# A recurrence, two mixtures of experts' products and a gated network on one core: the recurrence's first 14 chunks issued in a written order, loads without pads, one-hot rows by scalar operations

## The chip, the core and the metric

The kernel runs on one core of one Trainium2 chip. Its engines are PE (matrix products; PEld is its weight load), DVE (vector), ACT (scalar), POOL (GpSimd) and SP, which here only issues DMAs. The metric is the device time of one execution in microseconds, as a median of runs. A stage means a stretch of the span of one profiled execution.

## The reference

Three networks follow one another. The first is a gated linear recurrence over 768 steps in each of 4 x 8 heads of width 48; its output, 3072 rows of 384, goes through a top-2 mixture of 8 experts and then through a gated network.

```python
for t in range(S):
    state = f[:, :, t, :, None] * state + einsum('bhd,bhe->bhde', k[:, :, t], v[:, :, t])
    y[:, :, t] = einsum('bhd,bhde->bhe', q[:, :, t], state)
...
noisy_logits = x @ w_gate + log1p(exp(x @ w_noise)) * noise
top2 = argpartition(-noisy_logits, 2, axis=1)[:, :2]
out[mask] += top2_w[mask, k, None] * (maximum(x[mask] @ w1[e], 0.0) @ w2[e])
...
xn = x / sqrt(mean(x * x) + 1e-06) * rms_g
return (silu(xn @ w_gate) * (xn @ w_val)) @ w_out
```

## The kernel before

**The recurrence** is cut into 24 chunks of 128 steps, six for each batch; c is a chunk's place in its batch. Heads lie in pairs, 48 rows and 16 rows of pad for each, so that a chunk's keys and queries (tile kq) fill 128 partitions. `decay` clips the logits of the gates (tile ft, L331, DVE), takes two ACT functions and one DVE scan, which gives the running sums cs. `prep` makes the scaled keys KT and queries QT from cs (two ACT exponentials, one DVE product each; odd chunks' QT is POOL's). On PE a chunk has these steps, in this order: `scores` (masked on DVE into AM), `keys` of the next chunk (turned, evacuated by ACT to Ks), `rows` of the chunk before (its output and logits; ACT evacuates and SP stores x), `inter` (queries times the carried state Ss), a product of the identity with Ss (L395), which puts the old state into the sum of `state`, and `attend` (evacuated by ACT to yT). `carry` (L409) multiplies that sum by the chunk's decay on DVE and so makes the next Ss. A batch's first chunk has no `inter`, its last no `state`, and the `keys` of the last aren't needed.

**The experts.** The first 1024 tokens (chunks 0 to 7) are routed as soon as their rows are there: `router(0, NTA)` runs in nine steps between the chunks, popped by `safe()` three times in each iteration of `gla_stream`, from iteration 8 on. Its one-hot rows r_ol and r_rh are made for eight columns at a time (L541 to L545). The list of tokens (stoka) then feeds eight indirect DMAs on POOL (`fetch`, L721) for expert 0, four for each of two tiles; DVE turns each tile, ACT and DVE split it in two halves, and only then does the first product of an expert run (L645). From there the experts' units are woven between the steps of chunks 14 to 23, and go on alone afterwards. The other 2048 tokens are routed by the same code in 15 steps, one after each unit.

**Weights** come by SP (`start_loads`, L255) and are split in halves, whi by ACT (L209) and wlo by POOL (L211). Expert 0 has eight such parts, taken by `take_part` at the ends of iterations 6 to 13.

**What sets the order.** PE issues in the order in which the kernel is written, over the whole program. DVE, ACT and POOL do so only in the start, up to the first iteration; within the loop a scheduler puts their instructions in order when the kernel is built, by priority and readiness. Each engine then issues in that order and waits in it. SP issues DMAs in its own order; one that has to wait holds those behind it. Tiles with a fixed number of buffers (ft and kq have four) make a load wait until the last reader of its buffer is done. `paced` lets a fetch wait for the latest evacuation, and for the last `tick` (AM, yT or x) as long as there was none.

## Time and profile before

| | us |
|---|---|
| median of 3 runs (1107.76 to 1109.94) | 1109.58 |
| the profiled execution | 1118.4 |
| its span, first to last instruction | 1116.6 |
| PE busy (95% of the span) | 1060.1 |
| DVE busy (60%) | 666.1 |
| ACT busy (43%) | 482.1 |
| POOL busy (31%) | 350.5 |

The profiled execution took 0.8% longer than the median. Spans of 100 us are read from its trace as they stand. The chain that ended last is PE for 43% of the span, with the products of L645 for 42%; every other line in it holds 1% or less. A line of busy time by stretch shows how many microseconds each engine worked in it, the granted share of PE's full clock of 2.4 GHz (a mean of 1.00 and 0.50 within the stretch), the mean busy share of the 16 DMA engines and their rate. In a timeline the first number is the start and the second the duration; brackets give the engine's idle time before the instruction and what ended it.

### The profile page before, as it was taken

To read this page: it belongs to the slowest core of one execution; us is meant where nothing else is said; L and a number is where in the kernel's file an instruction comes from. 1 tells how busy PE (TensorE), PEld (TensorE's weight loads), DVE (VectorE), ACT (ScalarE), POOL (GpSimd) and SP (SyncE) were. 2 spreads that over 40 slices of the span, in tenths; PEclk is the share of its full clock that TensorE was granted. 3 is DMA by queue.
4 is the path that set the end of the run, shared out by engine and by line. 5 is a ranking of instruction groups with operands and counts; after the bars stand their busy time and mean duration, and the time that the engine had idled before them with its cause. 6 is when DMAs were issued, how large, how long until landed. Compare 5 with 4: busy or idle time off the path is not lost. (4 is left out here: it accounts for less than half of the span.)

```text
span 1116.6 us, 18933 instructions
## 1 busy us (share of the span) xinstructions
PE 1060.1 (95%) x7089; PEld 959.3 (86%) x7089; DVE 666.1 (60%) x1488; ACT 482.1 (43%) x1092; POOL 350.5 (31%) x373
## 2 busy tenths in 40 slices
PE   6986899989999999999999999999999999999997
PEld 4776698878989999999898988788888888888886
DVE  6886576498777654555675769735345444353332
ACT  6764555454565443444453555423223223232211
POOL 3553343344353434545545434120030020110000
PEclk8988899999999999999999999999999999999999
DMA  9996353456776543444443534120020110110000
GB/s 293 288 276 203 116 178 123 147 163 190 249 242 212 180 127 105 134 157 120 136 148 112 159 118 133 47 69 17 1 85 1 35 51 1 57 29 1 29 1 31
DMA packets 105255, 132.96 MB, mean 119 GB/s; under 512 B 9087, under 2 KB 81171, under 8 KB 105155
## 3 DMA queue, kind: packets, MB, share of 16 engines
q1 hardware_dynamic: 95587, 112.25, 31.6%
q0 software_dynamic: 9568, 19.43, 6.3%
q8 instruction: 57, 0.93, 0.4%
q14 instruction: 43, 0.35, 0.1%
HBM read 107.63 MB, written 24.02 MB: 118 GB/s over the span
## 5 line engine op out<-in xcount | busy, mean ns | idle before, releaser
L645 PE MATMUL bank<-xhi,whi 128*128 128x256 f32 (+8 forms) x1008 | 339.6, 337 | 14.5 <-DVE hlo L750 10.3
L645 PE MATMUL bank<-xlo,whi 128*128 128x256 f32 (+8 forms) x1008 | 336.2, 334 | 1.6 <-DVE xlo L633 1.6
L645 PE MATMUL bank<-xhi,wlo 128*128 128x256 f32 (+8 forms) x1008 | 335.8, 333 | 0.0
L645 PE MATMUL bank<-whi,hhi 128*128 128x384 f32 (+2 forms) x728 | 247.6, 340 | 4.2 <-ACT y L766 2.1
L645 PE MATMUL bank<-whi,hlo 128*128 128x384 f32 (+2 forms) x728 | 245.6, 337 | 0.0
L645 PE MATMUL bank<-wlo,hhi 128*128 128x384 f32 (+2 forms) x728 | 245.0, 337 | 0.0
L645 PEld LDWEIGHTS bank<-xhi,whi 128*128 128x128 f32 x1008 | 191.2, 190 | 39.4 <-DVE hlo L750 14.7
L645 PEld LDWEIGHTS bank<-xlo,whi 128*128 128x128 f32 x1008 | 191.2, 190 | 18.4 <-DVE xlo L633 2.7
L645 PEld LDWEIGHTS bank<-xhi,wlo 128*128 128x128 f32 x1008 | 191.4, 190 | 17.3
L721 POOL DMA_INDIRECT xg<-xd,stokr x139 | 135.6, 975 | 153.9 <-ACT hhi L749 124.3
L750 DVE SCALAR_TENSOR_TENSOR hlo<-bank,hhi 128x256 fp32r<-128x256 f32 (+7 forms) x192 | 83.2, 434 | 113.8 <-ACT hhi L749 96.0
L209 ACT ACTIVATE whi<-raw 128x256 fp32r<-128x256 f32 (+1 forms) x320 | 127.7, 451 | 40.1 <-DMA raw<-in_moe_w_dram 31.5
L645 PEld LDWEIGHTS bank<-whi,hhi 128*128 128x128 f32 (+2 forms) x728 | 133.4, 183 | 10.0 <-ACT y L766 2.7
L645 PEld LDWEIGHTS bank<-wlo,hhi 128*128 128x128 f32 (+2 forms) x728 | 133.4, 183 | 6.3
L211 DVE TENSOR_TENSOR wlo<-raw,whi 128x256 fp32r<-128x256 f32 (+1 forms) x282 | 126.6, 484 | 18.1 <-ACT whi L209 10.1
L645 PEld LDWEIGHTS bank<-whi,hlo 128*128 128x128 f32 (+2 forms) x728 | 132.8, 182 | 3.4
L749 ACT ACTIVATE hhi<-bank 128x256 fp32r<-128x256 f32 (+7 forms) x192 | 74.4, 388 | 131.9 <-PE bank L645 114.7
L840 DVE TENSOR_TENSOR sg<-bank,sg 128x512 f32<-128x512 f32 x72 | 49.7, 690 | 119.5 <-ACT sg L839 119.5
L791 POOL DMA_INDIRECT xg<-yd,slots x40 | 44.3, 1108 | 242.6 <-ACT hhi L843 207.6
L839 ACT ACTIVATE sg<-bank 128x512 f32<-128x512 f32 x72 | 43.2, 600 | 145.5 <-PE bank L645 136.8
L843 ACT ACTIVATE hhi<-sg 128x512 fp32r<-128x512 f32 x72 | 45.4, 631 | 115.8 <-DVE sg L841 115.6
L721 POOL DMA_INDIRECT xg<-xd,stoka x64 | 69.5, 1086 | 60.2 <-ACT hhi L749 47.7
(160 smaller groups left out, 1098.2 us busy)
## 6 DMA issues: line engine op xcount, KB each, us to landing
raw<-in_moe_w_dram SPq DMA_DIRECT2D x64, 768.0 KB
kq<-in_kq_dram SPq DMA_DIRECT2D x23, 512.0 KB
yd<-y SPq DMA_DIRECT2D x48, 192.0 KB
ft<-in_f_logit_dram SPq DMA_DIRECT2D x23, 256.0 KB
Vs<-in_v_dram SPq DMA_DIRECT2D x24, 192.0 KB
xd<-x SPq DMA_DIRECT2D x24, 192.0 KB
raw<-in_moe_w_gate_dram SPq DMA_DIRECT2D x6, 768.0 KB
raw<-in_moe_w_val_dram SPq DMA_DIRECT2D x6, 768.0 KB
```

The costliest lines, as they stand in the source:

```text
L209: nc.scalar.activation(hi[:, j], raw[:, j], AF.Copy)
L211: e.tensor_tensor(lo[:, j], raw[:, j], hi[:, j].bitcast(F32), op=OP.subtract)
L645: nc.tensor.matmul(o, a, b, start=start and i == 0, stop=stop and i == 2)
L721: paced(nc.gpsimd.indirect_dma_start(out=b.xg[i][:, k_], out_offset=None, in_=table, in_offset=bass.IndirectOffsetOnAxis(ap=rows_of[:, k_, ...
L749: mark[0] = nc.scalar.activation(hhi[:, :N], p[:, :N], AF.Relu).ins
L750: mark[1] = nc.vector.scalar_tensor_tensor(hlo[:, :N], p[:, :N], 0.0, hhi[:, :N].bitcast(F32), op0=OP.max, op1=OP.subtract).ins
L791: paced(nc.gpsimd.indirect_dma_start(out=y, out_offset=None, in_=ya if n < GROUP else yd, in_offset=bass.IndirectOffsetOnAxis(ap=at_, axis ...
L839: nc.scalar.activation(sg, ps[0], AF.Sigmoid)
L840: nc.vector.tensor_tensor(sg, ps[0], sg, op=OP.mult)
L843: mark[0] = nc.scalar.activation(hhi, sg, AF.Copy).ins
```

## The change

For the first 14 iterations PE, ACT, DVE and POOL each issue an iteration's instructions in the order in which they are written. That order is new: `prep` of chunk i+2 is spread over the iteration's steps, the gates of chunk i+4 and the sums of i+3 come at its end, the clip of chunk i+5 goes to POOL, and the part of the weights follows as the last. All QT are DVE's. The product of the identity with Ss is gone; `carry` adds the old state on DVE (su) and multiplies by the decay on POOL, or on DVE alone for a batch's first chunk. Loads of ft and kq leave the pads out once each of their five and four buffers has been filled, with two DMAs instead of one. The first weight loads go from iterations 4 and 6 to 2 and 4, the noise from 4 to 3, the zeros for the unused slots from 3 to 18. One-hot rows are made column by column with scalar operations on DVE, two for each column; the first router has two groups of eight columns as before, the second eight groups of four instead of four of eight, so that it has 19 steps. Idle places in the first router's plan are moved: step 8 comes one place later, in the middle of iteration 11. A fetch no longer waits for a tick.

```diff
-    NK, NV = AHEAD + 1, LOADS + 2
+    NK, NV = AHEAD + 1, 5
...
+    NF, NQ = 5, 4
+    Fs = [gp.tile([P, HP, P], F32, name=f"Fs{i}") for i in range(NF)]
+    Qs = [gp.tile([P, HP, 2, P], F32, name=f"Qs{i}") for i in range(NQ)]
+    def spans(first_round):
+        return [slice(0, P)] if first_round else [slice(0, D), slice(64, 64 + D)]
     def load_f(n, cuts=WHOLE):
         b, c = divmod(n, NCH)
-        t = st["f", n] = ld.tile([P, HP, P], F32, name="ft", bufs=4)
+        t = st["f", n] = Fs[n % NF]
         for s in cuts:
-            nc.sync.dma_start(t[:, s], f_logit[b, s, :, c * P:(c + 1) * P].rearrange(
-                "a d t -> d a t"))
+            for o in spans(n < NF):
+                nc.sync.dma_start(t[o, s], f_logit[b, s, o, c * P:(c + 1) * P].rearrange(
+                    "a d t -> d a t"))
 
     def load(n, which=("kq", "v")):
         b, c = divmod(n, NCH)
-        if which != ("v",):
-            st["kq", n] = ld.tile([P, HP, 2, P], F32, name="kq", bufs=4)
         for nm in which:
             if nm == "v":
                 nc.sync.dma_start(Vs[n % NV][:, :DM], v[b, c * P:(c + 1) * P])
             else:
-                i = {"k": slice(0, 1), "q": slice(1, 2), "kq": slice(0, 2)}[nm]
-                nc.sync.dma_start(st["kq", n][:, :, i], kq[b, :, i, :, c * P:(c + 1) * P].rearrange(
-                    "a i d t -> d a i t"))
-    def steps(fn, n, cuts=WHOLE):
+                t = st["kq", n] = Qs[n % NQ]
+                for o in spans(n < NQ):
+                    nc.sync.dma_start(t[o], kq[b, :, :, o, c * P:(c + 1) * P].rearrange(
+                        "a i d t -> d a i t"))
...
+    def clip(n, s=slice(0, HP), e=None):
 
 
         f = st["f", n][:, s]
+        (e or nc.vector).tensor_scalar(f, f, -GATES_MAX - 1.5, None, op0=OP.max)
+    def gates(n, s=slice(0, HP)):
         if s.start == 0:
             st["L", n] = wk.tile([P, HP, P], F32, name="L")
+        f, l = st["f", n][:, s], st["L", n][:, s]
+        nc.scalar.activation(l, f, AF.Exp, scale=-1.0)
+        nc.scalar.activation(l, l, AF.Ln, bias=1.0)
+    def sums(n, s=slice(0, HP)):
+        if s.start == 0:
             st["cs", n] = wk.tile([P, HP, P], F32, name="cs", bufs=4)
-        l, cs = st["L", n][:, s], st["cs", n][:, s]
-        nc.vector.tensor_scalar(f, f, -GATES_MAX - 1.5, None, op0=OP.max)
-        yield
-        nc.scalar.activation(l, f, AF.Exp, scale=-1.0)
-        yield
-        nc.scalar.activation(l, l, AF.Ln, bias=1.0)
-        yield
-        nc.vector.tensor_tensor_scan(cs.rearrange("p a t -> p (a t)"),
+        nc.vector.tensor_tensor_scan(st["cs", n][:, s].rearrange("p a t -> p (a t)"),
...
-        e = nc.gpsimd if n % 2 and banks[0] is BANK and n > 1 else nc.vector
-        e.tensor_tensor(st["QT", n][:, s], cs, st["kq", n][:, s, 1], op=OP.mult)
+        nc.vector.scalar_tensor_tensor(st["KT", n][:, s], Ek, KEYS_MAX, st["kq", n][:, s, 0],
+                                       op0=OP.min, op1=OP.mult)
+        yield
+        nc.scalar.activation(cs, cs, AF.Exp, scale=-1.0)
+        yield
+        nc.vector.tensor_tensor(st["QT", n][:, s], cs, st["kq", n][:, s, 1], op=OP.mult)
...
         st["pU", n] = pU = cut(bank("U"), HP, D)
-        if c:
-            nc.tensor.matmul(pU, ident, Ss[c % 2][:, :, :D], start=True, stop=False,
-                             skip_group_check=True)
         for a in range(HP):
             for g in range(2):
                 h = 2 * a + g
                 nc.tensor.matmul(pU[64 * g:64 * (g + 1), a], Ks[n % NK][:, h],
-                                 Vs[n % NV][:, h * D:(h + 1) * D], start=not c,
-                                 stop=True, skip_group_check=True)
+                                 Vs[n % NV][:, h * D:(h + 1) * D], start=True, stop=True,
+                                 skip_group_check=True)
 
     def carry(n):
 
         c = n % NCH
         if c == NCH - 1:
             return
-        st["C"] = nc.vector.tensor_tensor(Ss[(c + 1) % 2][:, :, :D], st["pU", n],
-                                          st["cs", n][:, :, P - 1:].to_broadcast([P, HP, D]),
-                                          op=OP.mult).ins
+        u, sn = st["pU", n], Ss[(c + 1) % 2][:, :, :D]
+        w = st["cs", n][:, :, P - 1:].to_broadcast([P, HP, D])
+        if c:
+            t = wk.tile([P, HP, D], F32, name="su", bufs=1)
+            nc.vector.tensor_tensor(t, u, Ss[c % 2][:, :, :D], op=OP.add)
+            st["C"] = nc.gpsimd.tensor_tensor(sn, t, w, op=OP.mult).ins
+        else:
+            nc.vector.tensor_tensor(sn, u, w, op=OP.mult)
...
-        hlf = rp.tile([P, 2, 2 * ng], F16, name="r_hf")
+        hlf = rp.tile([P, 2, 2 * ng], F32, name="r_hf")
         V.tensor_copy(hlf, hl)
         yield
         rh = rp.tile([P, 2 * ng, nst], F16, name="r_rh")
         ol = rp.tile([P, 2 * ng, P], F16, name="r_ol")
-        w = 8
+        w = 8 if n0 == 0 else 4
         for j in range(0, 2 * ng, w):
             o = slice(j, j + w)
-            V.tensor_tensor(ol[:, o], irowh[:, None, :].to_broadcast([P, w, P]),
-                            hlf[:, 1, o, None].to_broadcast([P, w, P]), op=OP.is_equal)
-            V.tensor_tensor(rh[:, o], irowh[:, None, :nst].to_broadcast([P, w, nst]),
-                            hlf[:, 0, o, None].to_broadcast([P, w, nst]), op=OP.is_equal)
-            V.tensor_tensor(rh[:, o], rh[:, o],
-                            names[:, 2 * n0 + j:2 * n0 + j + w, None].to_broadcast([P, w, nst]),
-                            op=OP.mult)
+            for k_ in range(j, j + w):
+                V.tensor_scalar(ol[:, k_], irowh, hlf[:, 1, k_:k_ + 1], None, op0=OP.is_equal)
+                m = 2 * n0 + k_
+                V.tensor_scalar(rh[:, k_], irowh[:, :nst], hlf[:, 0, k_:k_ + 1],
+                                names[:, m:m + 1], op0=OP.is_equal, op1=OP.mult)
             yield
...
-        m = mark[0] or st.get("tick")
+        m = mark[0]
         if m is not None:
...
+    ALL = {mybir.EngineType.PE, mybir.EngineType.Activation, mybir.EngineType.DVE,
+           mybir.EngineType.Pool}
     def gla_stream():
         def valid(n):
             return 0 <= n < NT
 
-        with tc.manual_schedule(engines={mybir.EngineType.PE, mybir.EngineType.Activation,
-                                         mybir.EngineType.DVE, mybir.EngineType.Pool}):
+        with tc.manual_schedule(engines=ALL):
             rest = constants()
             load_f(0, PARTS)
             next(rest)
             warm(10)
-            load(0, "kq")
+            load(0, ("kq",))
             load_f(1)
             load(0, ("v",))
-            load(1)
+            load(1, ("kq",))
             load_f(2)
+            load(1, ("v",))
+            load(2, ("kq",))
...
         for i in range(NT + 3):
             now[0] = i
             routing.extend(plan.get(i, []))
-            if i == 0:
-                for n in range(4, GATES + 1):
+            for n in ((4, 5, 6) if i == 0 else (i + 6,)):
+                if valid(n):
                     load_f(n)
-            if valid(i + GATES + 1):
-                load_f(i + GATES + 1)
-            if valid(i + LOADS):
-                load(i + LOADS)
+            if valid(i + 3):
+                load(i + 3, ("kq",))
+            if valid(i + 2):
+                load(i + 2, ("v",))
+            es = ExitStack()
+            if i < FETCH + 2:
+                es.enter_context(tc.manual_schedule(engines=ALL))
             if valid(i):
                 scores(i)
             safe()
             yield 1.1
             if i == 0:
                 run(prep, 1)
-                for n in range(2, GATES):
-                    after_prep(decay, n)
+            more = prep(i + AHEAD) if i and valid(i + AHEAD) else iter(())
+            next(more, None)
             if valid(i + 1):
                 keys(i + 1)
                 yield 1.1
+            next(more, None)
+            next(more, None)
             if valid(i - 1):
                 rows(i - 1)
             yield 1.2
             if valid(i):
                 inter(i)
             safe()
-            if valid(i + AHEAD):
-                run(prep, i + AHEAD)
+            next(more, None)
+            if i == 0:
+                run(decay, 2)
+                clip(3)
             if valid(i):
                 state(i)
-                with tc.high_priority(30):
+                with tc.high_priority(0 if i < FETCH + 2 else 30):
                     carry(i)
+            if i == 0:
+                gates(3)
+                run(prep, 2)
+                clip(4)
+            if valid(i + 4):
+                gates(i + 4)
+            if valid(i):
                 attend(i)
+            if valid(i + 3):
+                sums(i + 3)
+            if valid(i + 5):
+                clip(i + 5, e=nc.gpsimd if i < FETCH + 2 else nc.vector)
             safe()
-            if valid(i + GATES):
-                (after_prep if i < 14 else run)(decay, i + GATES)
+            if 6 <= i < 14:
+                take_part(0)
+            es.close()
             if i == 3:
+                nc.sync.dma_start(noise, moe_noise)
+                nc.sync.dma_start(gcol, moe2_rms_g)
+            if i in (2, 4):
+                start_loads()
+            if i == FETCH + 6:
                 nc.sync.dma_start(yd.rearrange("(e s) d -> s e d", e=E)[min(CAPS):],
                                   zeros[:, None, :].to_broadcast([SPAN - min(CAPS), E, DM]))
...
-            if i == 4:
-                nc.sync.dma_start(noise, moe_noise)
-                nc.sync.dma_start(gcol, moe2_rms_g)
-            if i in (4, 6):
-                start_loads()
-            if 6 <= i < 14:
-                take_part(0)
...
     def route(steps_):
-        with tc.high_priority(50):
-            return next(steps_, None)
+        return next(steps_, None)
 
     ahead = router(0, NTA, rpa)
     idle = lambda: None
-    for i in (8, 9):
+    for i in (8, 11):
         at(i, idle)
     for i in ROUTE:
         at(i, lambda: route(ahead))
+    at(9, idle)
...
-    for gap in (0, 0, 0, 0, 0, 1, 0, 0, 0, 0, 2, 1, 2, 2):
+    for gap in (0, 0, 0, 0, 0, 1, 0, 0, 0, 0, 0, 0, 0, 0, 2, 1, 2, 2):
```

## Rows read from the trace of the kernel before

**Rows 1.** Stretches: length, busy by engine (instructions), granted clock, DMA share, GB/s.

```profile
7.61:26.59 18.98, 12.35 (x131) 10.43 (x131) 13.52 (x23) 11.97 (x21) 6.54 (x21) 0.73 1.14 325
26.59:60.42 33.83, 31.57 (x430) 26.56 (x429) 28.74 (x39) 26.27 (x54) 17.13 (x21) 1.00 0.96 290
60.42:97.70 37.28, 27.91 (x321) 23.65 (x320) 31.33 (x87) 20.05 (x44) 13.93 (x17) 0.82 0.82 245
97.70:115.59 17.89, 13.00 (x156) 10.96 (x154) 10.89 (x19) 8.45 (x17) 10.35 (x10) 0.84 0.70 204
115.59:214.30 98.71, 93.45 (x979) 83.60 (x980) 60.31 (x105) 50.81 (x118) 40.43 (x47) 0.98 0.44 140
214.30:1116.60 902.30, 876.66 (x5065) 802.23 (x5063) 517.03 (x1206) 360.43 (x831) 259.96 (x239) 0.99 0.31 98
```

**Rows 2.** Timeline of PE, one chunk: start us, us, engine, line, operation, tiles.

```profile
101.75 1.16 PE L380 MATMUL scores<-QT,KT 48*128 48x128 f32 x16
102.84 0.65 PE L173 MATMUL bank<-ident,KT 128*128 128x128 f32 x4
103.33 1.04 PE L442 MATMUL bank<-columns,yT 128*128 128x112 f32 x8
104.31 1.09 PE L420 MATMUL bank<-QT,Ss 48*64 48x128 f32 x16
105.33 0.59 PE L395 MATMUL bank<-Ss,ident 128*128 128x192 f32 x2
105.85 0.67 PE L400 MATMUL bank<-Vs,Ks 128*64 128x48 f32 x16
106.35 1.05 PE L430 MATMUL bank<-AM,Vs 128*64 128x128 f32 x15
```

**Rows 3.** One line's instructions (ns minimum/median/maximum), then the timeline of both engines.

```profile
L331 DVE TENSOR_SCALAR ft<-ft x25: 293/419/1247, 3.1 to 119.8; 128x512 f32<-128x512 f32 x23, 128x256 f32<-128x256 f32 x2
30.75 1.28 POOL L359 TENSOR_TENSOR QT<-cs,kq 128x512 f32<-128x512 f32 x1
31.06 1.25 DVE L331 TENSOR_SCALAR ft<-ft 128x512 f32<-128x512 f32 x1
```

**Rows 4.** Weight halves on POOL before 115 us; a POOL copy.

```profile
L211 POOL TENSOR_TENSOR wlo<-raw,whi x20: 723/1004/1930, 42.1 to 76.5; 128x256 fp32r<-128x256 f32 x12, 128x384 fp32r<-128x384 f32 x8
7.55 0.69 POOL L107 COPY columns<-ident 128x384 f32<-128x384 f32 x1
```

**Rows 5.** Timeline of DVE, first router: step five, one-hot rows.

```profile
85.33 0.16 DVE L531 TENSOR_SCALAR r_hl<-slots 128x16 int32<-128x16 int32 x1
85.41 0.16 DVE L532 TENSOR_SCALAR r_hl<-slots 128x16 int32<-128x16 int32 x1
86.09 1.23 DVE L541 TENSOR_TENSOR r_ol<-irowh,r_hf 128x1024 f16<-128x1024 f16 x1
87.24 0.62 DVE L543 TENSOR_TENSOR r_rh<-irowh,r_hf 128x448 f16<-128x448 f16 x1
```

**Rows 6.** Groups of DVE: busy, mean ns; one scalar operation, 16 bits.

```profile
L116 DVE TENSOR_SCALAR sel<-sel,pcol 128x512 f16<-128x512 f16 x1 | 0.6, 581 | 0.0
```

**Rows 7.** Timeline from the token list to the first expert product.

```profile
97.21 0.28 DVE L611 TENSOR_SCALAR stoka<-bank,quad 128x64 int32<-128x64 f32 x1
100.45 1.41 POOL L721 DMA_INDIRECT xg<-xd,stoka  x1 [0.17 <-issue]
110.17 1.35 POOL L721 DMA_INDIRECT xg<-xd,stoka  x1 [0.30 <-issue]
115.59 0.58 PE L645 MATMUL bank<-xhi,whi 128*128 128x256 f32 x1 [1.86 <-ACT xhi L632]
```

**Rows 8.** Stretches as in group 1: second router, plain stretch.

```profile
241.00:259.00 18.00, 12.34 (x63) 11.07 (x62) 18.00 (x41) 8.07 (x21) 9.94 (x7) 0.81 0.41 125
300.00:400.00 100.00, 96.59 (x635) 93.34 (x634) 67.45 (x159) 55.22 (x147) 46.66 (x47) 1.00 0.62 203
```

**Rows 9.** Waits of PE after 116 us: us in total, times, longest.

```profile
PE bank L645 <- DVE hlo L750: 10.3, 10, 3.3
```

More of the change, by code (lines that the diff above doesn't have):

```diff
@@ L309, in steps, with run @@
+    def run(fn, n, cuts=WHOLE):
         for _ in zip(*[fn(n, s) for s in cuts]):
-            yield
-    def run(fn, n, cuts=WHOLE):
-        for _ in steps(fn, n, cuts):
-            pass
-    def after_prep(fn, n):
-        with tc.issue_after(st["e"]), tc.issue_after(st["K"]):
-            run(fn, n)
-    def decay(n, s):
+            pass
+    def clip(n, s=slice(0, HP), e=None):
         f = st["f", n][:, s]
+        (e or nc.vector).tensor_scalar(f, f, -GATES_MAX - 1.5, None, op0=OP.max)
@@ L332, in decay @@
+    def decay(n, s):
+        clip(n, s)
         yield
-        nc.scalar.activation(l, f, AF.Exp, scale=-1.0)
+        gates(n, s)
         yield
-        nc.scalar.activation(l, l, AF.Ln, bias=1.0)
+        sums(n, s)
         yield
-        nc.vector.tensor_tensor_scan(cs.rearrange("p a t -> p (a t)"),
-                                     chain[:, s].rearrange("p a t -> p (a t)"),
-                                     l.rearrange("p a t -> p (a t)"), 0.0,
-                                     op0=OP.mult, op1=OP.add)
@@ L341, in decay, with prep @@
-        yield
-    def prep(n, s):
+    def prep(n, s=slice(0, HP)):
         if s.start == 0:
@@ L383, in scores @@
         with tc.high_priority(30):
[L384 to L386 removed]
+            nc.vector.tensor_tensor(t, p.rearrange("p g a t -> p (g a) t"),
+                                    mask[:, None, :].to_broadcast([P, H, P]), op=OP.mult)
     def state(n):
[L390 to L391 removed]
+        if n % NCH == NCH - 1:
             return
         st["pU", n] = pU = cut(bank("U"), HP, D)
[L394 to L396 removed]
         for a in range(HP):
@@ L434, in attend @@
         with tc.high_priority(30):
-            st["tick"] = nc.scalar.activation(y, pY, AF.Copy).ins
+            nc.scalar.activation(y, pY, AF.Copy)
         st["yT", n] = y
@@ L443, in rows @@
         x = wk.tile([P, HP, NX], F32, name="x")
-        st["tick"] = nc.scalar.activation(x, p[:, :, :NX], AF.Copy).ins
+        nc.scalar.activation(x, p[:, :, :NX], AF.Copy)
         nc.sync.dma_start(xd[n * P:(n + 1) * P, :], x.rearrange("p a x -> p (a x)"))
@@ L1037, in gla_stream @@
             next(rest)
-        for n in range(2, LOADS):
-            load(n)
         for i in range(NT + 3):
```

16 lines of the change are left out of this document (5 added, 11 removed).

## The prediction

> **What bounds the kernel now.** I read the busy time by stretch first [rows 1]. From 115.59 us, where the first expert product runs [rows 7], to the end PE is busy for 970.11 of 1001.01 us: that part ends when PE's work does, and only less PE work or fewer PE stalls shorten it. Before 115.59 PE often waits, and the time is that of the recurrence and of the routing in front of the experts. The reader is to see four stretches there: the start up to the third chunk's scores (18.98 us), six chunks in which PE is busy for 31.57 of 33.83 us, four with the first router in which DVE is busy for 31.33 of 37.28 us and PE for 27.91 at a mean clock of 0.82, and 17.89 us from chunk 12's scores to the first expert product. After 116 us PE's largest wait is for DVE's hlo, 10.3 us in all [rows 9], and a good part of it lies in 241 to 259, where DVE is busy for 18.00 of 18.00 us with the second router's one-hot rows, and PE for 12.34 at a clock of 0.81 [rows 8].
>
> **The change, stretch by stretch.** The sum is made on the profiled execution, 1118.4 us with a span of 1116.6, and taken over to the median, 1109.58; 0.8% on a term of ten us is nothing.
>
> *The start.* The work up to chunk 2's scores is the same and DVE has it all in a row; the first round of loads keeps its pads. The zeros are gone from a stretch where the DMA share is 1.14, but the waits there are chains of DVE and ACT, so I count 0 (-1 to +1).
>
> *Six chunks bound by PE.* Its steps start at 101.75 (scores), 102.84, 103.33, 104.31, 105.33 (identity), 105.85, 106.35 (attend), and attend takes 1.05 [rows 2]: about 5.6 us a chunk, of which the identity holds 0.52. A chunk without it takes 5.07. Of six, one has no inter (1.02), one no state (0.50), one no keys (0.49), so six take 28.4 us; the old order's own floor is 28.4 + 4 x 0.52 = 30.5, and it took 33.83, with 3.3 us of waits. The new order spreads `prep` and puts the scan three chunks ahead, so some waits go: between 28.4 and 31.7, and I take 30.0, a gain of 3.8 (2.1 to 5.4). What covers it: ACT's 26.27 busy us in six chunks include weight halves, and fall with nothing; it would be next. The DMA share is 0.96 at 290 GB/s here. A chunk loads 960 KB and stores 192; without pads the loads fall to 768, so the transfers stay hidden in a stretch 11% shorter, but with little to spare. kq and ft now issue two DMAs each on SP; the SP queue stands one to three chunks ahead and hides them, unless a weight load (moved two iterations earlier) waits in front for its buffer. The noise, one iteration earlier, is hidden the same way.
>
> *Four chunks with the first router.* DVE sets the time. It loses four clips (0.42 each when alone [rows 3]), 1.7 us, and the carry's one DVE operation is replaced by one of the same shape; it gains the QT that POOL had, about 0.7 each for one or two chunks. One-hot rows: a group of eight columns takes 1.15 (starts 86.09, 87.24) and two operations of some 0.54 (0.62, less the 0.08 by which two in a row overlap) [rows 5], 2.2 us, and two groups 4.5. Now there are 16 pairs of scalar operations. Two small ones start 0.08 us apart [rows 5], the floor; 512 columns of 16 bits took 581 ns [rows 6] against 0.16 for 16 columns, which makes 0.26 for 128 and 0.19 for 56, or 0.18 and 0.11 from start to start. A pair costs 0.16 to 0.29; I take 0.24, 3.8 us. DVE's sum falls by 1.5 us. POOL's is 13.93 now and stays: two QT of 1.28 [rows 3] go, four clips and three multiplies by the decay come, and four weight parts fall here, which until now were all done by 76.5 [rows 4]. A clip on POOL has no row. A copy of 384 columns took 0.69, and part of that may be a wait, so 0.5 is the low end; the two-input QT of 512 columns took 1.28, the high end; I take 0.7, near the copy, which has one input as well. The multiply (192 columns) is below the 0.72 of the shortest wlo (256) [rows 4]; I take 0.6 (0.4 to 0.7).
>
> POOL's time isn't free to DVE. A clip on DVE that met POOL's QT took 1.25 us and ended at 32.31, 0.28 after the QT's end at 32.03 [rows 3]: it had waited for it whole. So what is written behind a weight half in time waits for it, and 32 short operations in a row can each meet one. I take 36.3 for the stretch, a gain of 1.0 (between +5, DVE's sum alone at PE's pace, and -4, if the waits fall between the short operations). The Trainium skill, SBUF — State Buffer, "SBUF: two separate sides", says that the port pair of DVE and GpSimd is locked for a whole instruction and that the loser fully blocks; that row agrees. It speaks against moving the clip: without the lock this stretch would gain some 2 us more.
>
> *From the token list to the first expert.* The list is ready at 97.21 + 0.28; the fetches start at 100.45 and 110.17 (first and eighth), so 1.39 apart, and the first product is 5.42 us after the last start [rows 7]. POOL's chain sets this. The tick's wait goes, which may save 1 to 3 us, but three halves of a weight part (0.72 each) of iteration 11 are written ahead of the first fetch, and a clip (0.7) and two halves (1.0 each, the median [rows 4]) ahead of the last. Queued behind them are the fetches, and the first expert waits for these. If the builder lets the next iteration's fetch pass a half that isn't ready, half of this vanishes. 17.89 becomes 20.4 (16.5 to 24): a loss of 2.5. The first step of the sum, the first expert's start, so falls from 115.6 to 0 + 3.8 + 1.0 - 2.5 = 2.3 us earlier, 113.3.
>
> *Chunks 14 to 23.* PE is busy for 93.45 of 98.71. Seven of the ten have the identity product: 7 x 0.52 = 3.6 us. The new carry has one more engine in its chain, POOL, which also queues the fetches of later experts, and these wait for an evacuation each; `inter` of the next chunk would wait, but it comes some expert products later. I take 3.4 (1.5 to 3.6).
>
> *The second router.* 241 to 259 loses 18.00 - 12.34 = 5.7 us of PE, and by the clock 0.19 x 18 = 3.4 more. PE was idle before its clock fell from 2.4 to 1.2 GHz for a while. A plain stretch leaves DVE 32.5 of 100 us [rows 8], with 635 products, 15 in a unit, so 42 units: 0.77 a unit. One group a unit (2.2) overdraws it by 1.4, four groups by 5.8, which is the idle time seen. Four pairs a unit cost 0.64 to 1.16: eight units are overdrawn by 0 to 3.1. At 0.24 it is 0.96 a unit, 1.5 in all, and the slack of the units in flight takes that up in part. I count a loss of 2.6 that stays, so a gain of 6.5 (2 to 9). The token lists come four units later; the weights that need them were asked for later than that. The Trainium skill, VectorE: DVE Perf Modes, "The perf-mode tier table", gives 693 ns for 2048 columns of a 16-bit scalar operation; an estimate by that page is 0.04 us for 128, so that only the starts would count, and the sum would be 1.5 us better. No row here shows that rate: 581 ns for 512 is slower.
>
> *Zeros.* They are 1536 KB on SP's queue between weight loads, at a DMA share of 0.44 and 140 GB/s; at the 290 GB/s of a full stretch they hold the queue for 5.4 us. Halves that wait for a load are hidden behind parts already split; I take -0.5 (-2 to 0).
>
> Sum: 2.3 + 3.4 + 6.5 - 0.5 = 11.7 us; 1109.6 - 11.7 = 1097.9, so 1098.
>
> **The rivals.** *POOL becomes the bound (slower).* Place: iteration 6 to the first expert. For: four things for POOL in an order that can't move within an iteration, and the lock. Against: its sum is only 13.93 of 37.28 now. Price: clips at 1.28, multiplies at 0.7, waits between the short operations. The six chunks gain 2.1, the router stretch loses 4, the fetches 6; with 2 from the second router, 2.4 from the identity and -0.5 for the zeros it is 4.0 slower: 1113.6. It decides as soon as POOL and DVE's two-input work together need over 5 us a chunk.
>
> *The front gains nothing (no change).* The first expert stays at 115.6 or comes 2 later, and pairs at 0.29 leave half of the second router's loss: -1.5 + 3.4 + 2 - 0.5 = 3.4 at best and about 1.7 in the middle: 1108. For it: the same DVE work in the same chain.
>
> *The pipeline holds (much faster).* Chunks at PE's pace: gains of 5.4, 5 and 1.4 in front, 3.6, 9 and 0: 24.4, so 1085. For it: PE's floor is 5.07 a chunk. Against: DVE's 31.33 busy us in the router stretch.
>
> **How the numbers follow.** My forecast 0.58, POOL as the bound 0.14, no change 0.15, much faster 0.13. A run of this kernel can't be told from no change within about 0.2%, 2.2 us. Faster: nearly all of the forecast (0.55), 0.13 and a third of the no-change case, 0.73 in all; within: 0.14; slower: 0.13. The forecast's terms alone range over some 1089 to 1107; to hold 8 in 10 the range takes in most of the two cases around it: 1086 to 1112.
>
> **What would show it.** In the profile after: no L395; scores of successive chunks 5.1 us apart up to the eighth; the first expert product near 113; in the second router PE idle under 2 us and its clock not at 1.2 GHz; 3.5 us less between the first expert product and the end of the recurrence. Wrong if the first expert comes after 117, with POOL busy without gaps from iteration 10 on; if PE waits for inter after 116 us; or if DVE stays full in the second router for over 18 us.

## The result, and the profile after

The changed kernel takes 1119.26 us (median of six, 1116.20 to 1120.54), the kernel before 1110.40 (1107.76 to 1111.51): a ratio of 1.0078 [1.0062, 1.0095], so 0.8% slower where 1.1% faster was forecast. Its profiled execution took 1119.37 us with a span of 1117.0, close to its median. The two profiles' spans differ by only 0.4 us, because the profiled execution of before took 1118.4, as this kernel does on three of the five chips of the experiments (medians of 1118 to 1121 us), against 1110 to 1111 on two: chips differ, and the stages below are set against further profiles of both.

Busy time by stretch, changed kernel; the stretches end at the scores of chunks 0, 2, 8 and 12, and stand against [rows 1]:

```profile
7.66:30.39 22.73, 12.88 (x130) 10.89 (x129) 13.63 (x23) 11.85 (x21) 5.89 (x22) 0.70 1.08 216
30.39:59.34 28.95, 28.75 (x422) 25.36 (x420) 23.27 (x34) 22.11 (x43) 18.67 (x19) 1.00 0.90 217
59.34:96.80 37.46, 26.52 (x315) 22.74 (x314) 32.00 (x108) 19.19 (x43) 20.94 (x23) 0.82 0.74 158
```

The first stretch is 3.8 us longer (5 to 6 in three further profiles, below), the second 4.9 shorter, the third as long as it was. The first expert product, which ended the front at 115.59 [rows 7], comes at 121.82:

```profile
121.82 0.58 PE L649 MATMUL bank<-xhi,whi 128*128 128x256 f32 x1 [13.04 <-ACT xhi L636]
```

So the front lost 6.2 us where it should have won 2.3, PE standing idle for 13.04 us at its end. What holds it up shows in the waits of SP's queue and of DVE. First the weight loads' waits before the change (20 to 116 us), then the changed kernel's (20 to 122, and DVE's from 57):

```profile
SPq L255 <- POOL hs L361: 1.2, 1, 1.2
SPq L255 <- POOL wlo L211: 0.8, 2, 0.6
```

```profile
SPq L255 <- POOL wlo L211: 16.5, 2, 8.3
SPq L255 <- POOL hs L367: 13.2, 2, 7.4
SPq L302 <- DMA raw<-in_moe_w_dram: 5.5, 3, 2.3
```

```profile
DVE KT L360 <- DMA Qs<-in_kq_dram: 9.4, 2, 5.7
```

The weight load (L255) waits 29.7 us on SP for POOL, where it waited 2.0. The timeline shows the chain twice:

```profile
63.08 2.10 POOL L211 TENSOR_TENSOR wlo<-raw,whi 128x256 fp32r<-128x256 f32 x3
65.20 0.56 SPq L255 DMA_DIRECT2D raw<-in_moe_w_dram  x1
71.36 0.82 SPq L313 DMA_DIRECT2D Qs<-in_kq_dram  x2
74.47 0.69 DVE L360 SCALAR_TENSOR_TENSOR KT<-Ek,Qs 128x512 f32<-128x512 f32 x1 [3.73 <-DMA Qs<-in_kq_dram]
...
100.51 1.00 POOL L211 TENSOR_TENSOR wlo<-raw,whi 128x256 fp32r<-128x256 f32 x1
101.53 0.55 SPq L255 DMA_DIRECT2D raw<-in_moe_w_dram  x1
108.17 1.31 SPq L313 DMA_DIRECT2D Qs<-in_kq_dram  x2
110.72 0.69 DVE L360 SCALAR_TENSOR_TENSOR KT<-Ek,Qs 128x512 f32<-128x512 f32 x1 [5.71 <-DMA Qs<-in_kq_dram]
```

POOL's weight half ends at 65.18 and 101.51; 0.02 us later SP issues the weight load that reuses its buffer, and only behind that the keys and queries; loads in between wait for the weight's landing besides (5.5 us in three). DVE needs the keys and queries one iteration later, in an order that it can't leave, and in the second case the tokens' turn for the first expert stands behind the waiting KT.

### The profile page after: what moved, and what is told of

It is laid out like the page before. It is cut to its first block, busy times and chain, and to the rows that moved or that the text cites. A ratio compares the mean times of both kernels' runs of the same rounds, so it can differ in the third digit from the quotient of the medians.

```text
span 1117.0 us, 19042 instructions
## 1 busy us (share of the span) xinstructions
PE 1050.4 (94%) x7057; PEld 954.7 (85%) x7057; DVE 673.8 (60%) x1559; ACT 482.0 (43%) x1092; POOL 371.1 (33%) x396
```

## The experiments

The theories named below: **Q**, SP's queue is held by the weight loads; **P**, POOL's clips and products set the pace; **S**, loads in two halves fill SP's queue with twice as many transfers; **T**, the bytes of the loads count; **O**, scalar one-hot operations cost more than assumed; **A**, the written order of ACT costs the start. First-expert times are compared across chips, ratios with care: the changed kernel gave 1.0067 [1.0043, 1.0092] and 1.0059 [1.0033, 1.0086] on two more chips, on both of which the kernel before takes 1110. One and the same edit (e1 and e7) gave 0.9986 on one chip and 1.0043 on another, with intervals that don't meet, so the ratios of e1 to e4 and e6, from chips on which the changed kernel wasn't timed, can't be set against these.

**Loads behind (e1 and e7).** `start_loads()` for a finished part is called after the next iteration's loads.

```diff
             if valid(i + 2):
                 load(i + 2, ("v",))
+            while owed:
+                owed.pop()
+                start_loads()
```

> One change to the changed kernel: in iterations 7 to 13 a weight load is issued behind the next iteration's loads of ft, kq and v instead of ahead of them. Theory Q (SP's queue: the weight load waits there for POOL's weight half, 29.7 us in all between 20 and 122 us, and the keys and queries stand behind it, for which DVE then waits 9.4 us): the waits of KT for kq fall from 9.4 to under 3 us, the first expert product comes from 121.8 to between 112 and 117, and the time falls by 5 to 9 us, to 1110 to 1114. Theory P (POOL's clips and products, and the port that it shares with DVE, set the pace): the first expert stays within 120 to 123 and the time within 2 us of 1119. Theory S (loads in two halves, so that the queue reaches its limit of transfers under way sooner): SP's waits for the landing of a weight load (6.4 us now) stay, and less than half of the gain of Q is seen, 1115 to 1118.

> The changed kernel, timed on the same chip as the kernel beside it: 1.004 to 1.008 of the kernel before, first expert at 121 to 123.

> The changed kernel with nothing but the weight loads of iterations 7 to 13 issued behind the next iteration's loads. Theory Q (the queue carries most of the loss): 4 to 8 us below the changed kernel on this chip, ratio to the kernel before 0.998 to 1.002, first expert at 115 to 117. Rival (the 0.9986 came from its chip, and what the queue gives back is taken by the fetches): within 2 us of the changed kernel.

Alone, e1 reached its first expert at 116.08 (ratio 0.9986 [0.9968, 1.0004], on a chip where the changed kernel wasn't timed). Side by side on another chip, the changed kernel (first row) and e7 (second):

```profile
124.05 0.58 PE L649 MATMUL bank<-xhi,whi 128*128 128x256 f32 x1 [11.72 <-ACT xhi L636]
```

```profile
117.22 0.58 PE L649 MATMUL bank<-xhi,whi 128*128 128x256 f32 x1 [11.30 <-ACT xhi L636]
```

6.8 us sooner, and DVE's wait for keys and queries is gone from the list. It stood there for the changed kernel on this chip; the weight load's own waits, e7's in the second block, stay (23.3 us) and cost the front little when nothing urgent is behind them:

```profile
DVE KT L360 <- DMA Qs<-in_kq_dram: 8.7, 2, 5.0
```

```profile
SPq L255 <- POOL wlo L211: 16.4, 2, 9.3
SPq L255 <- POOL hs L367: 6.9, 2, 3.6
```

The times are 1118.27 and 1114.71, 1.0059 and 1.0043 [1.0013, 1.0073]: 3.6 us less by the medians, 1.8 by the ratios, with intervals that overlap. Q is shown for the front; how much of the total it gives back is not.

**Pads (e2).** `spans` returns all 128 partitions, so that each load is one DMA.

```diff
-        return [slice(0, P)] if first_round else [slice(0, D), slice(64, 64 + D)]
+        return [slice(0, P)]
```

> One change to the changed kernel: every load of ft and kq takes the pads along, in one DMA, as before. Theory S (the halves hurt: twice as many transfers, 7 in an iteration instead of 5): the scores of chunk 2 come from 30.4 to 27 to 29, DVE's wait for kq falls from 9.4 to under 5, the time falls by 4 to 8 us. Theory Q: the weight load still waits for POOL's half, the keys behind it, so the time stays within 2 us of 1119. Theory T (bytes count, as the change supposes): a third more bytes in these loads make the front slower, by 2 to 6 us.

Chunk 2's scores came at 32.1, the first expert at 121.2; the waits of KT for kq vanished, but a wait of the scan took the place (4.8 us, behind POOL's Ss), and the weight load still waited 18.2 us for POOL. S foretold an earlier start, which didn't come; time on this chip equals the kernel before (1.0003 [0.9981, 1.0025]), and without the changed kernel beside it T can't be judged by time. Nor did the pads alone change: the builder put SP's DMAs in another order. The first two weight loads are issued at 20.0 and 32.6 us instead of 28.1 and 43.7, and the zeros far earlier, as the changed kernel (first) and e2 (second) show:

```profile
154.84 0.44 SPq L1110 DMA_DIRECT2D yd<-zeros  x1
```

```profile
38.91 0.43 SPq L1110 DMA_DIRECT2D yd<-zeros  x1
```

The stretch 30.4 to 59.3 tells something else, changed kernel first, e2 second:

```profile
30.40:59.30 28.90, 28.70 (x422) 25.36 (x420) 23.23 (x34) 22.07 (x43) 18.66 (x19) 1.00 0.90 217
```

```profile
30.40:59.30 28.90, 28.90 (x402) 25.66 (x401) 23.59 (x33) 21.33 (x42) 17.55 (x18) 0.95 0.99 308
```

PE is full in both. Of the 91 GB/s between them some 54 are the zeros (1536 KB in 28.9 us), so the rates don't show what the pads take. What a KB costs the 16 DMA engines does: 0.90 x 16 / 217, or 66 ns, without pads, and 51 with them (0.99 x 16 / 308), as in the kernel before (53, from the 0.96 and 290 GB/s of its six chunks [rows 1]). A chunk's 960 KB without pads so take the engines about as long as its 1152 KB with them, an estimate from these numbers; whether it is the 48 partitions or the two DMAs is not shown.

**Old one-hot rows (e3).** The three operations on many columns, in the new places (eight and four columns).

```diff
-            for k_ in range(j, j + w):
-                V.tensor_scalar(ol[:, k_], irowh, hlf[:, 1, k_:k_ + 1], None, op0=OP.is_equal)
...
+            V.tensor_tensor(ol[:, o], irowh[:, None, :].to_broadcast([P, w, P]),
+                            hlf[:, 1, o, None].to_broadcast([P, w, P]), op=OP.is_equal)
```

> One change to the changed kernel: one-hot rows again by operations on eight (first router) and four columns (second) at a time on 16-bit elements, in the same steps and places. Theory O (a scalar pair costs 0.36 us, as its starts show, not 0.24: 16 pairs take 5.9 us where two groups took 4.5, and 32 pairs 11.7 where eight half groups should take 9 to 10.5): the first router's last scores come 1 to 2 us earlier, waits of PE for hlo between 241 and 262 us fall, the time falls by 1 to 4 us. Rival (the scalar form is what eased the second router, as was forecast): slower by 2 to 5 us. Theory Q alone: within 1.5 us.

First expert at 120.4. From the 21st evacuation of a hidden tile (hlo) to the 51st, which the second router fills, it took 78.0 us; the changed kernel takes 78.7 to 79.7, the one before 79.0 to 79.8. c1, c2, b1 and b2 below, with old rows in groups of four, took 76.5 to 78.2, c3, whose units lie otherwise, 79.2. So the groups of four gain about 2, and the scalar form gives nearly all of that back: O holds by the stages; the ratio (1.0025 [1.0002, 1.0049]) has no changed kernel beside it.

**Clips on DVE (e4).**

```diff
-                clip(i + 5, e=nc.gpsimd if i < FETCH + 2 else nc.vector)
+                clip(i + 5, e=nc.vector)
```

> One change to the changed kernel: the clip of chunk i+5 on DVE instead of POOL, at the same place of the order. Theory P (a clip takes 1.48 us on POOL against 0.42 alone on DVE, and holds up what is behind it): POOL's busy time before 122 us falls by some 18 us, the first expert comes 3 to 6 us sooner, the time falls by 4 to 8 us. Theory Q: the weight half stands behind the clip on POOL, so a weight load that waits for it comes 1.5 us earlier, three times: 1 to 3 us faster. Rival (DVE is full where the router runs, and the clip belongs to POOL): slower by 1 to 3 us.

First expert at 121.3, ratio 1.0062 [1.0039, 1.0085]. From chunk 12's scores to the first expert POOL now works for 16.64 of 24.58 us, where the changed kernel's worked for 20.74 of 25.02:

```profile
96.80:121.82 25.02, 11.98 (x156) 10.71 (x153) 17.09 (x22) 13.00 (x28) 20.74 (x21) 0.70 0.59 134
```

```profile
96.77:121.35 24.58, 13.25 (x156) 11.14 (x153) 15.78 (x25) 13.04 (x28) 16.64 (x19) 0.78 0.62 137
```

The wait stays with a POOL that has time to spare: P alone explains nothing of the front. (Together with the loads it does something, below.)

**Attend early (e5).** In iteration 0 `attend(0)` is written ahead of the gates.

```diff
             if i == 0:
+                attend(0)
                 gates(3)
                 run(prep, 2)
```

> One change to the changed kernel: in iteration 0 the products of attend and their evacuation yT are written ahead of the gates of chunk 3 and the second prep, instead of behind them. Theory A (the written order of ACT is what costs the start 3.8 us: yT of chunk 0, whose products end at 17.2, stands at 24.4 behind gates that wait for two clips, and the products of rows wait for it for 3.5 us): rows starts by 19.5, the scores of chunk 2 come from 30.4 to 26 to 28, the time falls by 2 to 4 us. Rival (DVE's chain of clip, scan, keys and queries sets the start whatever ACT's order is): the scores of chunk 2 stay within 1 us of 30.4 and the time within 1 us.

The evacuation yT moved from 24.42 to 17.56, chunk 2's scores to 28.8, from 30.4 to 32.8 in the changed kernel's profiles. That is later than A's 26 to 28: from the scores of chunk 0 on it is 21.1 us, where the changed kernel takes 22.7 to 24.8 and the kernel before 18.7 to 19.0, so ACT's order is some half of the start's loss. The time stayed, 1.0059 against 1.0067 beside it, and the first expert came at 121.6. Set against the changed kernel on the same chip, e5 is 2.3 us ahead at the scores of chunk 8 (58.0 and 60.4) and 0.3 at those of chunk 12 (97.1 and 97.4), with this wait in between: A is right on the start in part, and its gain is lost again at the loads' waits.

```profile
DVE KT L360 <- DMA Qs<-in_kq_dram: 8.1, 2, 6.4
```

**Identity (e6).** The product is back, and the carry is DVE's alone.

```diff
+        if c:
+            nc.tensor.matmul(pU, ident, Ss[c % 2][:, :, :D], start=True, stop=False,
...
+        st["C"] = nc.vector.tensor_tensor(sn, u, w, op=OP.mult).ins
```

> One part of the change undone: the product of the identity with the old state is back on PE, the carry is one operation of DVE, and POOL's and DVE's two are gone. Theory I (the product costs PE 0.52 us a chunk wherever PE is the bound, which is from chunk 14 on): the stretch from the first expert's evacuation to the twentieth is 3 to 4 us longer, the first expert comes within 2 us of the changed kernel's 121.8, the time rises by 2 to 4 us. Rival (the carry over POOL hurts the front as much as the identity hurts PE): no change, within 1 us.

1130.43 us, 1.0099 [1.0077, 1.0120]. The six chunks of the second stretch took 31.41 us, all of it PE's, where four profiles of the changed kernel have 28.95 to 29.21:

```profile
33.07:64.48 31.41, 31.41 (x430) 27.25 (x428) 24.63 (x35) 22.82 (x44) 12.73 (x15) 0.97 0.79 189
```

From the first to the 21st evacuation it took 99.9 us, the changed kernel 95.5 to 99.0. So leaving out the product does gain, some 2.4 us in the six chunks and some 3 in chunks 14 to 23; what that is of the time isn't shown, since the changed kernel wasn't timed on this chip.

**Together (c1 and c2).** Loads behind, old rows and attend early in one; the clips on DVE besides in the other; the changed kernel beside them.

> The changed kernel itself once more, as the measure for the runs beside it, since chips differ. If its ratio to the kernel before is again 1.006 to 1.010, the other ratios of this study can be set against 1.0078; if it lies near 1.000 on a chip where the kernel before is slower, the gains are to be read against this run alone.

> Three changes to the changed kernel together: weight loads behind the next iteration's loads, one-hot rows as before, attend early in iteration 0. If they add up (5.7 us for the loads by the first expert's start, 1.4 for the first router's rows, 2 to 4 for the start, 1 to 2 in the second router): the first expert at 110 to 113, and the time 9 to 13 us below the changed kernel. Rival (what is gained in front is waited for in the fetches, whose chain goes by POOL): the first expert at 114 to 117, 5 to 8 us below.

> The three changes of the kernel beside it, and the clips on DVE. Theory P2 (once the loads are out of the way POOL's clip decides the first expert: behind the fetches and a weight half it comes at 110.2, gates on ACT wait for it, and the tokens' half xhi, ready to be made at 108.5, stands behind these till 113.2): 3 to 5 us below the kernel beside it, the first expert at 106 to 110. Rival (DVE is full in the router's stretch, five clips more there): no gain, within 1.5 us of it or slower.

On one chip: changed kernel 1119.55, e5 1118.90, c1 1109.40 (0.9991 [0.9964, 1.0017]), c2 1110.21 (0.9981 [0.9953, 1.0008]). Ten us come back, clear of the intervals, though e5 alone gave none. The two profiles differ by 13.7 us, of which only 3.9 lie ahead of the first expert product; 4.8 lie between the first and the 21st evacuation and 1.8 in the second router. The recurrence as a whole comes earlier, its last scores at 200.1 instead of 209.4. That the stalls lie one behind the other and each swallows what is gained ahead of it is seen in e5; how much of the ten us it explains is argued, as neither e3 nor e7 was timed on this chip. The clips bring the first expert from 117.5 to 114.7 and the time nothing. In the kernel with the loads behind, ACT's gates wait for a clip that POOL has in line after eight fetches and a weight half, and xhi waits behind the gates (e1's timeline):

```profile
107.62 1.96 POOL L211 TENSOR_TENSOR wlo<-raw,whi 128x384 fp32r<-128x384 f32 x2
107.85 0.69 DVE L736 STREAM_TRANSPOSE xt<-xg 128x384 f32<-128x384 f32 x1 [2.48 <-DMA xg<-xd,stoka]
110.15 1.48 POOL L324 TENSOR_SCALAR Fs<-Fs 128x512 f32<-128x512 f32 x1
111.67 0.63 ACT L331 ACTIVATE L<-Fs 128x512 f32<-128x512 f32 x1 [6.70 <-POOL Fs L324]
113.24 0.51 ACT L636 ACTIVATE xhi<-xt 128x384 fp32r<-128x384 f32 x1
```

**Where the two kernels differ on one chip.** Further profiles of the kernel before, and both on one chip:

> The kernel before itself, one more profiled execution. The profile that the prediction read took 1118.4 us, 0.8% above the median, and the difference of the two medians (8.9 us) does not show between the two profiles (1116.6 and 1117.0). Theory F (that execution had a slow front, and the kernel before usually reaches its first expert sooner): the first expert product comes at 107 to 111 here instead of 115.6, and the span is 1106 to 1112. Rival (the excess lay in the experts, from the clock): the first expert at 114 to 117, and the stretch behind it 990 to 996 instead of 1001.

> The kernel before once more, to tell what varies between its executions from what is fixed: by theory F its first expert product comes at 107 to 111, by the rival at 114 to 117; the scores of chunk 2, where only the written order of the start acts, should be within 0.5 us of 26.6 in both.

> The kernel before, beside a profile of the changed kernel on the same chip. Theory M (the chip's loads: the front of both kernels waits for transfers, so a chip on which these are quicker shortens the front, and more so where loads are asked for early): where the run takes 1110, the first expert comes 3 to 8 us earlier than the 114.7 to 116.3 of the three profiles so far. Theory K (the chip's clock: fewer falls of TensorE's clock): the front is within 1.5 us of 115.6, the mean clock is higher by 0.005 or more, and the stretch behind the first expert is shorter by 5 to 9. Where the run takes 1118 to 1120 again, both are as before.

> The changed kernel on the chip of the kernel beside it. If chips differ in both kernels alike, it takes 7 to 11 us more than that one, with the first expert 5 to 8 us later, the stretch from there to the twentieth evacuation 3 to 4 shorter and the second router 0 to 2 shorter, and the rest equal; if the difference of the kernels goes with the chip, it takes within 3 us of it on a chip where that takes 1118.

F falls: the first expert of the kernel before came at 116.3, 114.7 and 114.3. On one chip (1116.67 and 1124.10 us), kernel before, then changed:

```profile
114.33 0.58 PE L645 MATMUL bank<-xhi,whi 128*128 128x256 f32 x1 [2.38 <-ACT xhi L632]
```

```profile
122.11 0.58 PE L649 MATMUL bank<-xhi,whi 128*128 128x256 f32 x1 [7.02 <-ACT xhi L636]
```

The first, 21st and 51st evacuations, in the same order:

```profile
118.21 0.42 DVE L750 SCALAR_TENSOR_TENSOR hlo<-bank,hhi 128x256 fp32r<-128x256 f32 x1 [1.98 <-ACT hhi L749]
216.49 0.42 DVE L750 SCALAR_TENSOR_TENSOR hlo<-bank,hhi 128x256 fp32r<-128x256 f32 x1 [1.14 <-ACT hhi L749]
295.45 0.42 DVE L750 SCALAR_TENSOR_TENSOR hlo<-bank,hhi 128x256 fp32r<-128x256 f32 x1
```

```profile
125.83 0.42 DVE L754 SCALAR_TENSOR_TENSOR hlo<-bank,hhi 128x256 fp32r<-128x256 f32 x1 [2.58 <-ACT hhi L753]
224.80 0.42 DVE L754 SCALAR_TENSOR_TENSOR hlo<-bank,hhi 128x256 fp32r<-128x256 f32 x1 [1.14 <-ACT hhi L753]
303.69 0.42 DVE L754 SCALAR_TENSOR_TENSOR hlo<-bank,hhi 128x256 fp32r<-128x256 f32 x1
```

7.8 us lie in front and none behind: 98.3 and 99.0 us to the 21st evacuation, 79.0 and 78.9 to the 51st. All four profiles of the kernel before are of executions of 1117 to 1120 us; none shows where it saves the rest when it takes 1110. Why the kernel before takes 1110 on some chips and 1118 to 1121 on others, while the changed one takes 1118 to 1124, stays open: M and K are not told apart, since the chip on which both were profiled is not of the first kind.

**What to keep.** b1 and b2 start from the kernel before, c3 from c2.

```diff
-        if c:
+        if c and n < 14:
             nc.tensor.matmul(pU, ident, Ss[c % 2][:, :, :D], start=True, stop=False,
...
-        w = 8
+        w = 8 if n0 == 0 else 4
```

> The kernel before with two parts of the change alone: without the identity product (carry by a sum on DVE and a product on POOL), and with the second router's one-hot rows in eight groups of four columns, by the old operations on many columns. Theory I+G: 3.0 to 3.6 us less from the first expert to the twentieth unit, 1.5 to 3 less in the second router: faster than before by 3 to 7 us (0.3 to 0.6%). Rival (the scheduler puts POOL's carry behind fetches and weight halves, and inter waits): within 1.5 us of before, or slower.

> The kernel before with the identity product left out from chunk 14 on alone, where PE is the bound, and the second router's one-hot rows in eight groups of four columns by the old operations. With the identity left out everywhere the first expert came 5 to 6 us late, and the rest was 5 to 7 us shorter. Theory I+G: the first expert stays at 114 to 117, the stretch to the twentieth evacuation is 2.5 to 3.5 shorter, the second router 1.5 to 3: 4 to 7 us faster than before (0.994 to 0.996). Rival (the front came late there because of the groups or by the scheduler's mood, not because of the carry): the first expert at 119 or later, no faster than 0.998.

> The changed kernel with loads behind, one-hot rows by the old operations, attend early, clips on DVE, and the two turns of the first tokens one iteration later. Without the last, PE waited 11.3 us for the first expert, with chunk 14's other steps written behind that. Theory W (the fetches land at the same time whatever PE does, so a chunk's work goes into that wait): the first expert within 2 us of 114.7, but the end of the recurrence 3 to 5 us earlier: 3 to 5 us below the kernel without it, so 0.993 to 0.996 of the kernel before where that takes 1110. Rival (the chunk's own operations on DVE and ACT stand ahead of the turns and push them back by as much): first expert at 118 to 120, no gain.

b1, without the identity everywhere: 0.9978 [0.9962, 0.9994], first expert at 121.5: the new carry costs the front, as b2 shows, which leaves it out there. b2, the edit shown, without it only from chunk 14 on: first expert at 115.3, 1113.68 against 1119.09 us, 0.9947 [0.9923, 0.9972]. c3, with the turns of the first tokens one iteration later: first expert at 120.3, as its rival said, yet the recurrence's last scores at 197.9 (201.4 in c2, 202.5 to 204.6 before the change), 1112.56 us, 0.9948 [0.9930, 0.9967]; c2 wasn't timed beside it. Both are 0.5% faster than the kernel before on the same chip, where the changed kernel's one run took 1124.10. On a chip where the kernel before takes 1110 neither was timed.

## Why the prediction was wrong

**The start: wrong.** I counted 0 (-1 to +1) and it lost 3.8; in the three further profiles the stretch took 24.0 to 24.8 us, for 18.7 to 19.0 before, with a mean granted clock of 0.53 to 0.65 (0.73 before [rows 1]). I said that the work was the same and that DVE had it in a row; I didn't walk ACT's new order. Changed kernel:

```profile
20.86 1.94 POOL L324 TENSOR_SCALAR Fs<-Fs 128x512 f32<-128x512 f32 x1
21.36 0.83 DVE L324 TENSOR_SCALAR Fs<-Fs 128x512 f32<-128x512 f32 x1
22.23 0.63 ACT L331 ACTIVATE L<-Fs 128x512 f32<-128x512 f32 x1 [1.97 <-DVE Fs L324]
24.42 0.58 ACT L441 ACTIVATE yT<-bank 128x512 f32<-128x512 f32 x1
25.09 2.02 PE L448 MATMUL bank<-columns,yT 128*128 128x112 f32 x8 [3.54 <-issue]
```

yT stands behind gates that wait for a clip on DVE, itself stretched from 0.42 to 0.83 beside POOL's. Written early (e5), it gives back some half.

**Six chunks bound by PE: right.** 33.83 became 28.95, a gain of 4.9 for 3.8 (2.1 to 5.4); about half of it is the identity's, by e6. A full chunk follows the one before in the 5.07 us foretold. The loads stayed hidden as I said, but not by the bytes saved: a KB took the DMA engines 66 ns instead of 53, and with pads (e2) the stretch took 29.05.

**Four chunks with the first router: right by its range, wrong by its cause.** 37.28 became 37.46. A scalar pair costs 0.36 to 0.37 us from start to start, above my 0.29 at the top:

```profile
84.32 0.24 DVE L548 TENSOR_SCALAR r_ol<-irowh,r_hf 128x128 f16<-128x128 f16 x1
84.48 0.29 DVE L550 TENSOR_SCALAR r_rh<-irowh,r_hf,names 128x56 f16<-128x56 f16 x1
84.68 0.24 DVE L548 TENSOR_SCALAR r_ol<-irowh,r_hf 128x128 f16<-128x128 f16 x1
```

16 pairs take 5.9 us, not 3.8. The operation on 128 columns came as scaled (0.24 us, 0.16 from start to start, for 0.26 and 0.18). The other was mis-sized: 56 columns, compared and then multiplied, take 0.29 and 0.20 for my 0.19 and 0.11, which I scaled from operations with a single step; and I took less than my own sum of 0.29. By the rate alone of the Trainium skill, VectorE: DVE Perf Modes, "The perf-mode tier table", an estimate for 128 columns is 0.04 us; the row says 0.24. POOL's 13.93 us, which I let stay, became 20.94; my own items (2.8 for clips, 1.8 for multiplies, less 2.6 for QT) already added 2.

The long stall in this stretch, and the longer one in the next, was the weight load on SP. That is the step that failed. I had the loads of keys and queries hidden by an SP queue that stands one to three chunks ahead, "unless a weight load ... waits in front for its buffer", and put that condition at nothing without a reason. It came true: the weight loads waited 29.7 us on SP for POOL, DVE 9.4 us for the keys and queries behind them, and with the weight loads out of the way (e7) the first expert came 6.8 us sooner.

**From the token list to the first expert: right in sign, three times too small.** From chunk 12's scores 17.89 became 25.02, a loss of 7.1 for 2.5 (the range ended at 24). The clip took 1.48 us, outside my 0.5 to 1.28, and 5.7 us were again DVE's wait for keys and queries. The Trainium skill, GPSIMD Engine Reference, "Engine selection", calls operations with one input roughly line-rate on GpSimd; here the same clip takes 1.48 there and 0.42 on DVE [rows 3], and an estimate by that rule would have been near my low end.

```profile
L324 POOL TENSOR_SCALAR Fs<-Fs x14: 1477/1482/1937, 20.9 to 116.5; 128x512 f32<-128x512 f32 x14
```

**Chunks 14 to 23: right in kind, half the size.** From the first to the 21st evacuation four profiles of the kernel before took 98.3 to 99.1 us, four of the changed one 95.5 to 99.0, about 1.8 less for 3.4 (e6 puts the product's part at some 3). In b2 on one chip PE waits longer for hlo than in the kernel before (11.4 and 8.1 us between 123 and 400), which may be the rest, as DVE got the sum; that is argued, not shown. PE's clock is at half, 1.2 GHz, from 121.82 to 125 and at 0.65 in the mean to 129, after 13 us of idling; before the change it was at half from 115.59 to 120, after 3.3 us of work in 7.6. Changed kernel, then before:

```profile
121.82:125.00 3.18, 2.67 (x11) 2.38 (x12) 1.03 (x2) 2.54 (x5) 0.19 (x1) 0.50 1.04 309
125.00:129.00 4.00, 4.00 (x27) 3.87 (x28) 1.08 (x3) 1.67 (x4) 2.71 (x3) 0.65 0.85 133
```

```profile
108.00:115.59 7.59, 3.29 (x17) 2.39 (x16) 5.49 (x11) 2.81 (x6) 3.04 (x4) 0.62 0.52 156
115.59:120.00 4.41, 3.63 (x15) 3.35 (x16) 2.43 (x5) 2.10 (x5) 0.48 (x2) 0.50 0.21 61
```

**The second router: wrong.** About 0.5 for 6.5. From 242 to 262 DVE is full, for 20 us where I had named 18 as a sign of being wrong, with PE idle for 4.9:

```profile
242.00:262.00 20.00, 15.12 (x100) 13.38 (x100) 20.00 (x82) 9.14 (x24) 7.82 (x8) 1.00 0.57 175
```

At 0.365 four pairs are 1.46 a unit against 0.77 of slack; the forecast's 0.96 is where it fell. The clock did stay up here, as said, but in two of the other three profiles of the changed kernel its mean from 242 to 262 is 0.91. One long wait became many short ones (PE's waits for hlo 12.3 us in 17, for 10.3 in 10 [rows 9]).

**Zeros:** no run told them apart.

Of the rivals, POOL as the bound came nearest in time, 1113.6, and the order on POOL does matter, but through SP's queue and not by POOL being full: POOL is busy 20.94 of 37.46 us there and 20.74 of 25.02 in the next stretch, and with its clips gone (e4) the first expert comes no sooner. The sum missed by some 20 us: 8.5 in front, 6 in the second router, 1.6 in chunks 14 to 23; where the other 4 or 5 lie isn't shown, since no execution of the kernel before at 1110 was profiled.

## What to carry to other kernels

When an engine's order is written out by hand, walk every queue that waits for it, the DMA queue first: a load that needs a buffer freed at the end of an iteration must not stand ahead of loads needed at the beginning of the next. Stalls in a row hide each other, so an edit that gains nothing alone can be worth its size once the stall behind it is gone. Price a short operation by the start-to-start time of its own kind, not by another kind scaled down. Before one edit is read as one cause, see whether the builder kept the order of everything else.

## What the hardware showed unexpectedly

With loads of 2 x 48 partitions in two DMAs a KB took the DMA engines 66 ns, with whole ones 51 to 53: a fifth of the loads' bytes left out saved hardly any of the engines' time. A clip of 512 columns takes 1.48 us on POOL and 0.42 on DVE. POOL's product of 192 columns (L415) takes 0.51 us alone and up to 1.36 beside DVE's scan. The same program differs by 0.8% between chips at median clocks of 0.979 and 0.980 on the two where it takes 1110 and 0.977 to 0.979 on the three others.
